# Attention and a soft mixture of experts on one core: longer q and k loads, transposes on quarters, one-bank tail tiles, zero products on TensorE

## The chip, the cores and the metric

The kernel runs on one core of a Trainium2 chip. The metric is the device time of one execution in microseconds. Times are medians of several executions; "span" is the part of an execution that the profile covers, about 1.8 us shorter than its time. All ratios are the mean time of one kernel's fast runs over the mean of the other's fast runs in the same rounds, so they are not quite the ratio of the medians quoted beside them.

Terms: TensorE makes the matrix products and writes them to tiles in PSUM, a memory of eight banks here; VectorE and ScalarE copy them out, which is called eviction. A load "lands" when its last bytes have arrived. A packet is one piece of a transfer, as the page counts them. The transfers are spread over 16 DMA engines; "DMA share" is their mean busy share, and "clock" the part of its full clock that TensorE was granted (PEclk in the strips, in tenths).

## The reference

```python
# attention: q, k, v are (4, 8, 768, 64); heads 0, 2, 6 see all earlier keys,
# the others the first 4 keys and the last 64
scores = scale * np.matmul(q, k.transpose(0, 1, 3, 2))
scores = np.where(mask, scores, -1e9)
a = softmax(scores)
x = np.matmul(a, v)                      # -> (3072 tokens, 512)
# soft mixture of experts, 8 experts with 4 slots each
logits = x @ phi                         # (3072, 32)
slot_input = softmax_over_tokens(logits).T @ x
for e in range(8):                       # w1[e]: 512 x 1024, w2[e]: 1024 x 512
    slot_out[e] = np.maximum(slot_input[e] @ w1[e], 0.0) @ w2[e]
return softmax_over_slots(logits) @ slot_out        # (3072, 512), f32
```

Nothing of the output can be written before the softmax over all tokens is done and all eight second-layer weights have been used. The inputs are 52.5 MB of f32, cast to bf16 on the way in (26.25 MB); the output is 6.29 MB.

## The kernel before

The parts that the change and the argument touch, with cuts marked `# ...`. `NP` is 16 pairs of heads; `trp`, `pvp` and `scp` are PSUM pools of two tiles each (one bank, one bank, two banks, eight banks in all).

```python
    def load_qk(n, which):
        # ...
        t = raw.tile([P, 2, 384], BF16, tag="r" + which, name="r" + which)
        nc.gpsimd.dma_start(t, src[b, h:h + 2].rearrange("h (p s) d -> p h (s d)", s=6))

    def transposes(n, which):
        # ...
        for s in range(6):
            for hh in range(2):
                nc.tensor.transpose(tp[64 * hh:64 * hh + 64, s, :], src[:, hh, 64 * s:64 * s + 64], ident)
    # ...
    for h in range(H):      # far masks, before the first exponential
        nc.scalar.copy(fmask[:, h], r1[:, h:h + 1]...to_broadcast([P, 4, 66]))
        nc.scalar.copy(fmask[:, h, 0], r0[:, h:h + 1].to_broadcast([P, 66]))
    # ... sixteen pairs of attention, with weights loaded between q, k and v; then the experts' tail ...
    sp = pvp.tile([P, DM], F32, tag="pv", name="sp")
    for e4, gs in ((0, (0, 1, 2, 3)), (1, (0, 1)), (1, (2,)), (1, (3,))):
        second(e4, gs)                              # the last group waits for the last weights
    V.tensor_copy(slot_out[:, :256], sp[:, :256])
    nc.scalar.copy(slot_out[:, 256:], sp[:, 256:])

    for t, rows in enumerate((1, 1, 2, 4, 4, 4, 4, 4)):
        ot = single([P, rows, DM], F32, f"ot{t}", tag=f"w1_{t}")
        for y in range(0, rows, 2):
            op = scp.tile([P, 2, DM], F32, tag="sc", name="op")
            for x in range(min(2, rows)):
                nc.tensor.matmul(op[:, x], er[r], slot_out, start=True, stop=True)
                if r % 2:
                    nc.scalar.activation(ot[:, y + x], op[:, x], ACT.Copy, scale=rrow[:, r:r + 1])
                else:
                    V.tensor_scalar(ot[:, y + x], op[:, x], rrow[:, r:r + 1], None, op0=ALU.mult)
                r += 1
        nc.sync.dma_start(ov[:, r - rows:r, :], ot)
```

The softmax here doesn't subtract the row's maximum and nothing guards it: scores larger than these inputs give would overflow.

## Time and profile before

| | before |
|---|---|
| time, median (lowest to highest) | 169.53 us (168.79 to 169.67, 3 runs) |
| span of the profiled run | 168.9 us (an execution of 170.73 us) |
| attention's last exponential and products end | about 117 us |
| last weights land | 139.1 us |
| slot_out ready | 141.05 us |
| output written, end | 168.9 us |

Read it as two stages that cannot overlap: loads until the last weights have landed, and the output after slot_out. Attention lies inside the first. What each stage costs is set by what ends last in it, not by the busiest engine: the page's first part (below: engine, busy us, share of the span, instructions) has no engine above 72%.

```profile
PE 121.2 (72%) x1751; PEld 72.0 (43%) x1752; DVE 102.0 (60%) x226; ACT 113.7 (67%) x162; POOL 58.6 (35%) x89
```

The wait of the output queue's own engine (SPq; line 523 is where the program ends) for its last transfer is short, 3.4 us: it is handed its last rows late.

```profile
SPq L523 <- DMA out_dram<-ot: 3.4, 1, 3.4
```

### The profile page before, as it was taken

The page shows a single profiled execution, that of the slowest core. Times are in us where ns is not written, and L with a number is a line of the kernel's source. Part 1 is how long each engine was busy: PE and PEld are TensorE (multiplying, and loading weights), DVE is VectorE, ACT ScalarE, POOL GpSimd, SP SyncE. Part 2 cuts the span into 40 slices and gives each one's busy share as a digit, 9 for nine tenths or more (in the row PEclk, how much of TensorE's full clock was granted, in tenths as well). Part 3 has the DMA queues.
Part 4 walks back from the last instruction along what each step waited for, and adds up shares of the span by engine and source line. Part 5 has one row for each costly group of instructions (what it writes and reads, how often), then busy time and mean ns, then how long its engine had stood idle before and what let it go on. Part 6 is the DMA issues. An engine that isn't in the chain of part 4 may idle for free.

```text
span 168.9 us, 4098 instructions
## 1 busy us (share of the span) xinstructions
PE 121.2 (72%) x1751; PEld 72.0 (43%) x1752; DVE 102.0 (60%) x226; ACT 113.7 (67%) x162; POOL 58.6 (35%) x89
## 2 busy tenths in 40 slices
PE   0445988987769989869989887988587964565430
PEld 0332555654436556546565545556233721111100
DVE  2846579999657889755898765887224104434410
ACT  3599899999778999978999979792303202334330
POOL 7974475463644445544453615006100000000000
PEclk9999999999999999995999997899858997555555
DMA  3999999999999999999999999999999920556665
GB/s 46 150 175 187 200 194 197 190 215 189 202 196 196 209 196 192 201 201 200 201 196 192 211 191 212 213 215 216 210 213 217 205 50 28 220 237 260 248 278 219
DMA packets 39985, 32.80 MB, mean 194 GB/s; under 512 B 26656, under 2 KB 34848, under 8 KB 39328
## 3 DMA queue, kind: packets, MB, share of 16 engines
q0 software_dynamic: 38672, 26.25, 104.4%
q1 hardware_dynamic: 1296, 6.30, 9.2%
q8 instruction: 13, 0.21, 0.5%
q14 instruction: 4, 0.03, 0.0%
HBM read 52.50 MB, written 6.29 MB: 348 GB/s over the span
## 4 chain that ended last, share of the span: by engine, by line
DMA 36%; PE 8%; DVE 8%; issue 3%; POOL 1%; ACT 1%; POOLq 0%
DMA w<-in_moe_w_dram 29%; DMA rk<-in_k_dram 7%; PE op L486 7%; DVE ot L490 5%; DVE pT L183 1%; PE sp L470 1%; DVE Tq L147 1%; POOL vb L114 0%; ACT ot L488 0%; DVE xb L201 0%; POOL w L127 0%; POOL w L391 0%; PE pv L192 0%; DVE xT L210 0%; DVE slot_out L476 0%
## 5 line engine op out<-in xcount | busy, mean ns | idle before, releaser
L171 ACT ACTIVATE pT<-sc 128x1024 bf16<-128x1024 f32 (+1 forms) x96 | 83.6, 928 | 9.3 <-PE sc L166 8.6
L166 PE MATMUL sc<-Tq,Tk 64*128 64x256 bf16 (+3 forms) x320 | 37.4, 300 | 16.6 <-ACT Tk L150 8.9
L192 PEld LDWEIGHTS <-pT 128*128 128x128 bf16 x672 | 25.1, 100 | 11.2 <-issue 7.9
L183 DVE TENSOR_TENSOR pT<-pT,msk 128x1024 bf16<-128x1024 bf16 (+1 forms) x48 | 29.3, 639 | 0.2 <-ACT pT L171 0.2
L192 PE MATMUL pv<-vb,pT 128*128 128x65 bf16 x352 | 27.7, 198 | 0.0
L192 PE MATMUL pv<-vf,pT 128*128 128x65 bf16 x320 | 25.3, 197 | 0.0
L114 POOL DMA_DIRECT2D vb<-in_v_dram x16 | 16.5, 1034 | 22.8 <-PE sc L166 7.7
L166 PEld LDWEIGHTS <-Tk 64*128 64x128 bf16 x320 | 12.1, 96 | 27.4 <-ACT Tk L150 11.6
L486 PE MATMUL op<-slot_out,expT 128*128 128x512 bf16 x23 | 11.7, 599 | 11.0 <-DVE ot L490 10.1
L147 DVE COPY Tq<-tpq 128x768 bf16<-128x768 bf16 x16 | 15.3, 957 | 5.5 <-PE tpq L140 5.5
L201 DVE TENSOR_TENSOR xb<-pv,rs 128x384 bf16<-128x384 f32 x32 | 17.8, 558 | 1.1
L488 ACT ACTIVATE ot<-op,rrow 128x512 f32<-128x512 f32 x12 | 8.3, 688 | 14.4 <-PE op L486 14.4
L200 DVE RECIPROCAL rs<-pv 128x6 f32<-128x6 f32 x32 | 6.2, 194 | 18.9 <-PE pv L192 18.7
L490 DVE TENSOR_SCALAR ot<-op,rrow 128x512 f32<-128x512 f32 x12 | 9.0, 751 | 12.7 <-PE op L486 12.7
L150 ACT COPY Tk<-tpk 128x768 bf16<-128x768 bf16 x16 | 13.0, 814 | 3.8 <-PE tpk L140 3.8
L108 POOL DMA_DIRECT2D rk<-in_k_dram x16 | 11.5, 719 | 7.4 <-PE sc L166 3.2
L140 PE MATMUL tpk<-ident,rk 128*64 128x128 bf16 x192 | 9.4, 240 | 5.5 <-DMA rk<-in_k_dram 4.9
L108 POOL DMA_DIRECT2D rq<-in_q_dram x16 | 11.5, 717 | 2.1 <-DMA vb<-in_v_dram 1.9
L140 PE MATMUL tpq<-ident,rq 128*64 128x128 bf16 x192 | 10.0, 251 | 3.0 <-DMA rq<-in_q_dram 3.0
L127 POOL DMA_DIRECT2D w<-in_moe_w_dram x16 | 9.0, 561 | 8.1 <-DMA w<-in_moe_w_dram 7.2
L486 PEld LDWEIGHTS <-expT 128*128 128x128 bf16 x24 | 3.8, 157 | 17.6 <-issue 17.5
L140 PEld LDWEIGHTS <-rk 128*64 128x64 bf16 x192 | 6.7, 120 | 9.5 <-DMA rk<-in_k_dram 4.9
(70 smaller groups left out, 118.1 us busy)
## 6 DMA issues: line engine op xcount, KB each, us to landing
w<-in_moe_w_dram POOLq DMA_DIRECT2D x32, 512.0 KB, 12.5
out_dram<-ot SPq DMA_DIRECT2D x5, 1024.0 KB, 3.9
rk<-in_k_dram POOLq DMA_DIRECT2D x16, 192.0 KB, 11.5
rq<-in_q_dram POOLq DMA_DIRECT2D x16, 192.0 KB, 11.5
vb<-in_v_dram POOLq DMA_DIRECT2D x16, 192.0 KB, 10.8
out_dram<-ot SPq DMA_DIRECT2D x2, 256.0 KB, 2.2
out_dram<-ot SPq DMA_DIRECT2D x1, 512.0 KB, 2.6
phi<-in_moe_phi_dram POOLq DMA_DIRECT2D x1, 32.0 KB, 10.4
```

What stands on the lines that cost most here:

```text
L108: nc.gpsimd.dma_start(t, src[b, h:h + 2].rearrange("h (p s) d -> p h (s d)", s=6))
L114: nc.gpsimd.dma_start(vbs[n % 5].rearrange("p h j d -> p (h j) d")[:, :, :D], a.rearrange("h (j p) d -> p (h j) d", p=P))
L140: nc.tensor.transpose(tp[64 * hh:64 * hh + 64, s, :], src[:, hh, 64 * s:64 * s + 64], ident)
L147: nc.vector.tensor_copy(o, i)
L150: nc.scalar.copy(o, i)
L166: nc.tensor.matmul(sc[:, hh, at:at + 128 * cnt], kT[n][po:po + 64, j * 128:(j + 1) * 128], qT[n][po:po + 64, i0 * 128:(i0 + cnt) * 128], s ...
L171: nc.scalar.activation(pT[n][:, :, o:o + ln], sc[:, :, :ln], ACT.Exp, scale=scale)
L183: nc.vector.tensor_mul(x, x, m)
L192: nc.tensor.matmul(pv[n][:, i % 3, hh, :], pT[n][:, hh, o:o + 128], vv[:, hh, j, :D + 1], start=(j == 0), stop=(j == i))
L201: nc.vector.tensor_mul(xb[b][:, 3 * half:3 * half + 3, h * D:(h + 2) * D].rearrange("p i (h d) -> p i h d", h=2), pv[n][:, :, :, :64], rs. ...
L486: nc.tensor.matmul(op[:, x], er[r], slot_out, start=True, stop=True)
L490: V.tensor_scalar(ot[:, y + x], op[:, x], rrow[:, r:r + 1], None, op0=ALU.mult)
```

## The change

Its intent: fewer and longer DMA runs for q and k (128 rows of 3 KB, two heads on two halves of the partitions, so that each head's transposes use a diagonal quarter of the array); loads issued in the order of need; the far masks taken off ScalarE, which had to finish them before its first exponential; in the tail one-bank tiles, so that two engines and two neighbours in time don't share a tile; and products with zeros where TensorE would wait, to hold its clock.

```diff
-        t = raw.tile([P, 2, 384], BF16, tag="r" + which, name="r" + which)
-        nc.gpsimd.dma_start(t, src[b, h:h + 2].rearrange("h (p s) d -> p h (s d)", s=6))
+        t = raw.tile([P, S], BF16, tag="r" + which, name="r" + which)
+        nc.gpsimd.dma_start(t, src[b, h:h + 2].rearrange("h (p s) d -> (h p) (s d)", s=12))
 ...
-        for s in range(6):
+        for s in range(12):
             for hh in range(2):
-                nc.tensor.transpose(tp[64 * hh:64 * hh + 64, s, :], src[:, hh, 64 * s:64 * s + 64], ident)
+                po = slice(64 * hh, 64 * hh + 64)
+                nc.tensor.transpose(tp[po, s, :], src[po, 64 * s:64 * s + 64], ident[po, po])
 ... (order of loads: q before k, v and weights after them)
+    def keep_busy(t, count):
+        for _ in range(count):
+            nc.tensor.matmul(t, zero[:, :P], zero, start=True, stop=True)
 ... (31 such products: 9 + 10 around the start, 12 in the tail)
-        nc.scalar.copy(fmask[:, h], r1[:, h:h + 1]...)          # all 8 heads at the start
+        V.tensor_copy(fmask[:, h:h + 2, 1:], r1[:, h:h + 2]...)  # 2 heads, as needed
 ... (slot sums in three bf16 tiles; hp, transposes of h and sp in one-bank tiles;
      the second layer in two halves of 256 columns; row sums rp after second(1, (0, 1)))
-    V.tensor_copy(slot_out[:, :256], sp[:, :256])
-    nc.scalar.copy(slot_out[:, 256:], sp[:, 256:])
+    V.tensor_copy(slot_out[:, :256], sp[0])
+    nc.scalar.copy(slot_out[:, 256:], sp[1])
 ...
-        for y in range(0, rows, 2):
-            op = scp.tile([P, 2, DM], F32, tag="sc", name="op")
-            for x in range(min(2, rows)):
-                nc.tensor.matmul(op[:, x], er[r], slot_out, start=True, stop=True)
+        for y in range(rows):
+            op = bank((1, 2, 0)[r % 3])        # one bank, six tiles in rotation
+            nc.tensor.matmul(op, er[r], slot_out, start=True, stop=True)
```

More of the change, by code (lines that the diff above doesn't have):

```diff
@@ L87 @@
     slot_acc = single([P, DM], F32, "slot_acc")
-    slot_bf = single([P, 2, DM], BF16, "slot_bf")
+    slot_bf = [single([P, DM], BF16, f"slot_bf{x}") for x in range(3)]
     xT = single([P, 4, S], BF16, "xT")
@@ L112, in load_v @@
         b, h = n // 4, 2 * (n % 4)
-        a = v[b, h:h + 2]
         nc.gpsimd.dma_start(vbs[n % 5].rearrange("p h j d -> p (h j) d")[:, :, :D],
-                            a.rearrange("h (j p) d -> p (h j) d", p=P))
+                            v[b, h:h + 2].rearrange("h (j p) d -> p (h j) d", p=P))
     wi = [0]
@@ L136, in transposes @@
         src = (qraw if which == "q" else kraw)[n]
-        tp = trp.tile([P, 6, P], BF16, tag="tr", name="tp" + which)
-        for s in range(6):
+        tp = trp.tile([P, 12, 64], BF16, tag="tr", name="tp" + which)
+        for s in range(12):
             for hh in range(2):
-                nc.tensor.transpose(tp[64 * hh:64 * hh + 64, s, :], src[:, hh, 64 * s:64 * s + 64], ident)
+                po = slice(64 * hh, 64 * hh + 64)
+                nc.tensor.transpose(tp[po, s, :], src[po, 64 * s:64 * s + 64], ident[po, po])
         return tp
@@ L144, in evac @@
         dst = qkT.tile([P, S], BF16, tag="T" + which, name="T" + which)
-        o, i = dst.rearrange("c (p s) -> c p s", s=6), tp.rearrange("c s p -> c p s")
+        o, i = dst.rearrange("c (p s) -> c p s", s=12), tp.rearrange("c s p -> c p s")
         if which == "q":
@@ L237, in dispatch_mm @@
     def dispatch_mm(b, i0=0, i1=6):
-        if i0 == 0:
-            sps[b] = pvp.tile([P, DM], F32, tag="pv", name="slp")
+        sp = sps[b, i0] = pvp.tile([P, DM], F32, tag="pv", name="slp")
         for i in range(i0, i1):
-            g = i % 4
-            nc.tensor.matmul(sps[b][32 * g:32 * g + 32, :], elgs[b][:, i, :], xb[b][:, i, :],
-                             start=(i < 4), stop=(i + 4 >= 6))
+            g = (i - i0) % 4
+            nc.tensor.matmul(sp[32 * g:32 * g + 32, :], elgs[b][:, i, :], xb[b][:, i, :],
+                             start=(i - i0 < 4), stop=(i + 4 >= i1))
     def slot_sum(b):
-        sp = sps[b]
+        sp = sps[b, 0]
         if b == 0:
@@ L249, in slot_sum @@
         elif b == B - 2:
-            nc.vector.tensor_add(slot_bf[:, 0], slot_acc, sp)
-        elif b < B - 1:
+            nc.vector.tensor_add(slot_bf[0], slot_acc, sp)
+        else:
             nc.vector.tensor_add(slot_acc, slot_acc, sp)
-        else:
-            nc.scalar.copy(slot_bf[:, 1, :256], sp[:, :256])
-            nc.vector.tensor_copy(slot_bf[:, 1, 256:], sp[:, 256:])
     load_qk(0, "k")
@@ L264 @@
                    allow_small_or_imprecise_dtypes=True)
+    load_qk(1, "q")
+    load_qk(1, "k")
     load_v(0)
-    load_qk(1, "k")
-    load_qk(1, "q")
+    w_load(1)
+    load_qk(2, "q")
+    load_qk(2, "k")
     load_v(1)
     w_load(1)
-    load_qk(2, "k")
-    load_qk(2, "q")
     load_v(2)
-    w_load(1)
     V = nc.vector
+    zero = single([P, 512], BF16, "zero")
+    V.memset(zero, 0.0)
+    def keep_busy(t, count):
+        for _ in range(count):
+            nc.tensor.matmul(t, zero[:, :P], zero, start=True, stop=True)
+    idle = pvp.tile([P, 512], F32, tag="pv", name="idle")
+    keep_busy(idle, 9)
     V.tensor_single_scalar(ident, diff[:, :P], 0.0, op=ALU.is_equal)
@@ L297, with far_mask @@
         evac(0, which, transposes(0, which))
+        keep_busy(idle, 2)
     for h in range(2):
         head_mask(h)
-    V.memset(vbs[0][:, :, :, D:], 1.0)
-    for h in range(H):
-        nc.scalar.copy(fmask[:, h], r1[:, h:h + 1].rearrange("p (o d) -> p o d", o=1).to_broadcast([P, 4, 66]))
-        nc.scalar.copy(fmask[:, h, 0], r0[:, h:h + 1].to_broadcast([P, 66]))
-    for t in vbs[1:]:
+    def far_mask(n):
+        h = 2 * n
+        V.tensor_copy(fmask[:, h:h + 2, 1:], r1[:, h:h + 2].rearrange("p (h a d) -> p h a d", a=1, d=1).to_broadcast([P, 2, 3, 66]))
+        V.tensor_copy(fmask[:, h:h + 2, 0], r0[:, h:h + 2].rearrange("p (h d) -> p h d", d=1).to_broadcast([P, 2, 66]))
+    for t in vbs:
         V.memset(t[:, :, :, D:], 1.0)
+    far_mask(0)
     def setup_late():
@@ L319 @@
         if n + 3 < NP:
+            load_qk(n + 3, "q")
             load_qk(n + 3, "k")
-            load_qk(n + 3, "q")
             load_v(n + 3)
@@ L332 @@
         scores(n, 0)
+        if n == 0:
+            keep_busy(idle, 2)
         if n >= 1:
@@ L347 @@
         scores(n, 2)
+        if n == 0:
+            keep_busy(idle, 2)
         if n >= 1:
@@ L361 @@
         scores(n, 4)
+        if n == 0:
+            keep_busy(idle, 2)
         if n + 1 < NP:
@@ L378 @@
         if n < 3:
+            far_mask(n + 1)
             for h in (2 * n + 2, 2 * n + 3):
@@ L387 @@
     w2s[5] = single([P, 8, DM], BF16, "w2_5", tag="msk")
-    def w2_late(e):
-        for half in range(2):
-            nc.gpsimd.dma_start(w2s[e][:, 4 * half:4 * half + 4], w2v[e][:, 4 * half:4 * half + 4])
-    w2_late(5)
+    nc.gpsimd.dma_start(w2s[5], w2v[5])
     w2s[6] = ptp.tile([P, 8, DM], BF16, tag="pT", name="w2_6")
-    w2_late(6)
+    nc.gpsimd.dma_start(w2s[6], w2v[6])
     last, bl = NP - 1, B - 1
@@ L407 @@
     w2s[7] = ptp.tile([P, 8, DM], BF16, tag="pT", name="w2_7")
-    w2_late(7)
+    for half in range(2):
+        nc.gpsimd.dma_start(w2s[7][:, 4 * half:4 * half + 4], w2v[7][:, 4 * half:4 * half + 4])
+    idle = scp.tile([P, 512], F32, tag="sc", name="idle")
     x_transpose(last, 0, 3)
+    keep_busy(idle, 2)
     logits_mm(bl, (3,), (0,))
@@ L412 @@
     x_transpose(last, 3, 6)
+    keep_busy(idle, 1)
     logits_mm(bl, (3,), (1,))
     logits_exp(bl, 1)
+    keep_busy(idle, 1)
     exp_tokens(bl, 0, 3)
+    keep_busy(idle, 1)
     dispatch_mm(bl, 0, 3)
+    keep_busy(idle, 1)
     exp_tokens(bl, 3, 6)
+    keep_busy(idle, 1)
     dispatch_mm(bl, 3, 6)
-    slot_sum(bl)
+    keep_busy(idle, 3)
+    V.tensor_copy(slot_bf[1][:96], sps[bl, 0][:96])
+    V.tensor_copy(slot_bf[2][:96], sps[bl, 3][:96])
     csum = small.tile([P, 1], F32, tag="cs", name="csum")
@@ L424, with bank @@
     V.tensor_scalar(emask, emask, rcol, None, op0=ALU.mult)
-    sip = trp.tile([P, 4, ES], F32, tag="tr", name="sip")
-    sv = [slot_bf[:, x].rearrange("p (di do) -> p do di", do=4) for x in range(2)]
+    def bank(t, shape=(P, 512), dt=F32):
+        pool, tag = ((scp, "sc"), (trp, "tr"), (pvp, "pv"))[t]
+        return pool.tile(list(shape), dt, tag=tag, name="bank")
+    sip = bank(1, (P, 4, ES))
+    sv = [t.rearrange("p (di do) -> p do di", do=4) for t in slot_bf]
     for do in range(4):
-        for x in range(2):
-            nc.tensor.matmul(sip[:, do], sv[x][:, do], sum4, start=(x == 0), stop=(x == 1))
+        for x in range(3):
+            np_ = 96 if x else P
+            nc.tensor.matmul(sip[:, do], sv[x][:np_, do], sum4[:np_], start=(x == 0), stop=(x == 2))
@@ L432 @@
     V.tensor_copy(siT, sip)
+    keep_busy(idle, 2)
     hs = []
     for e4 in range(2):
-        hp = scp.tile([P, 2, 512], F32, tag="sc", name="hp")
+        t = xp.tile([P, 2, 512], BF16, tag="xb", name="hs")
         for c in range(2):
+            hp = bank(0 if e4 == 0 else 2)
             for do in range(4):
                 for g in range(4):
-                    nc.tensor.matmul(hp[32 * g:32 * g + 32, c], siT[:, do],
+                    nc.tensor.matmul(hp[32 * g:32 * g + 32], siT[:, do],
@@ L440 @@
                                      w1s[4 * e4 + g][:, do, c * 512:(c + 1) * 512],
                                      start=(do == 0), stop=(do == 3))
-        t = xp.tile([P, 2, 512], BF16, tag="xb", name="hs")
-        nc.scalar.activation(t[:, 0], hp[:, 0], ACT.Relu, scale=emask[:, e4:e4 + 1])
-        V.tensor_scalar(t[:, 1], hp[:, 1], emask[:, e4:e4 + 1], 0.0, op0=ALU.mult, op1=ALU.max)
+            if c == 0:
+                nc.scalar.activation(t[:, 0], hp, ACT.Relu, scale=emask[:, e4:e4 + 1])
+            else:
+                V.tensor_scalar(t[:, 1], hp, emask[:, e4:e4 + 1], 0.0, op0=ALU.mult, op1=ALU.max)
@@ L445 @@
         hs.append(t.rearrange("p c f -> p (c f)").rearrange("p (fi fo) -> p fo fi", fo=8))
-    hT = []
-    for e4 in range(2):
-        tp = trp.tile([P, 8, P], BF16, tag="tr", name="tph")
-        for fo in range(8):
-            nc.tensor.transpose(tp[:, fo, :], hs[e4][:, fo, :], ident)
-        t = qkT.tile([P, 8, P], BF16, tag="hT", name="hT")
-        if e4 == 0:
-            V.tensor_copy(t, tp)
-        else:
-            nc.scalar.copy(t, tp)
-        hT.append(t)
-    rp = trp.tile([P, 24], F32, tag="tr", name="rp")
+    hT = {}
@@ new lines, in turn, with second @@
+    def turn(e4):
+        t = qkT.tile([P, 8, P], BF16, tag="T" + "qk"[e4], name="hT")
+        for x in range(2):
+            tp = bank(1, (P, 4, P), BF16)
+            for fo in range(4):
+                nc.tensor.transpose(tp[:, fo, :], hs[e4][:, 4 * x + fo, :], ident)
+            if x:
+                nc.scalar.copy(t[:, 4:], tp)
+            else:
+                V.tensor_copy(t[:, :4], tp)
+        hT[e4] = t
+    sp = [bank(0, (P, 256)) for x in range(2)]
+    def second(e4, gs):
+        for fo in range(8):
+            for x in range(2):
+                for g in gs:
+                    nc.tensor.matmul(sp[x][32 * g:32 * g + 32, :], hT[e4][:, fo, 32 * g:32 * g + 32],
+                                     w2s[4 * e4 + g][:, fo, 256 * x:256 * x + 256],
+                                     start=(e4 == 0 and fo == 0), stop=(e4 == 1 and fo == 7))
@@ L458 @@
+    turn(0)
+    second(0, (0, 1, 2, 3))
+    turn(1)
+    second(1, (0, 1))
+    rp = bank(1, (P, 24))
     er = []
@@ L463 @@
     V.reciprocal(rrow, rp)
-    sp = pvp.tile([P, DM], F32, tag="pv", name="sp")
-    def second(e4, gs):
-        for fo in range(8):
-            for g in gs:
-                nc.tensor.matmul(sp[32 * g:32 * g + 32, :], hT[e4][:, fo, 32 * g:32 * g + 32],
-                                 w2s[4 * e4 + g][:, fo, :],
-                                 start=(e4 == 0 and fo == 0), stop=(e4 == 1 and fo == 7))
-    for e4, gs in ((0, (0, 1, 2, 3)), (1, (0, 1)), (1, (2,)), (1, (3,))):
-        second(e4, gs)
-    V.tensor_copy(slot_out[:, :256], sp[:, :256])
-    nc.scalar.copy(slot_out[:, 256:], sp[:, 256:])
+    second(1, (2,))
+    second(1, (3,))
+    V.tensor_copy(slot_out[:, :256], sp[0])
+    nc.scalar.copy(slot_out[:, 256:], sp[1])
     ov = out.rearrange("(p r) d -> p r d", r=24)
@@ L482 @@
         ot = single([P, rows, DM], F32, f"ot{t}", tag=f"w1_{t}")
-        for y in range(0, rows, 2):
-            op = scp.tile([P, 2, DM], F32, tag="sc", name="op")
-            for x in range(min(2, rows)):
-                nc.tensor.matmul(op[:, x], er[r], slot_out, start=True, stop=True)
-                if r % 2:
-                    nc.scalar.activation(ot[:, y + x], op[:, x], ACT.Copy, scale=rrow[:, r:r + 1])
-                else:
-                    V.tensor_scalar(ot[:, y + x], op[:, x], rrow[:, r:r + 1], None, op0=ALU.mult)
-                r += 1
+        for y in range(rows):
+            op = bank((1, 2, 0)[r % 3])
+            nc.tensor.matmul(op, er[r], slot_out, start=True, stop=True)
+            if r % 2:
+                nc.scalar.activation(ot[:, y], op, ACT.Copy, scale=rrow[:, r:r + 1])
+            else:
+                V.tensor_scalar(ot[:, y], op, rrow[:, r:r + 1], None, op0=ALU.mult)
+            r += 1
         nc.sync.dma_start(ov[:, r - rows:r, :], ot)
```

## The prediction

> **What bounds the kernel now.** I read the page first: its strip of 40 slices (each 4.2 us) and the shares of the chain of work that ended last.
>
> ```profile
> PEclk9999999999999999995999997899858997555555
> DMA  3999999999999999999999999999999920556665
> GB/s 46 150 175 187 200 194 197 190 215 189 202 196 196 209 196 192 201 201 200 201 196 192 211 191 212 213 215 216 210 213 217 205 50 28 220 237 260 248 278 219
> ...
> DMA 36%; PE 8%; DVE 8%; issue 3%; POOL 1%; ACT 1%; POOLq 0%
> ```
>
> The DMA engines are full from slice 2 to slice 32, then almost empty for two slices, then 50 to 60% busy to the end. So there are two stages: loading (to about 139 us), limited by transfers, and writing out (141 us on), limited by something else. The chain in order of time names the links:
>
> ```profile
> 87.81 13.67 DMA w<-in_moe_w_dram
> ...
> 101.77 15.23 DMA w<-in_moe_w_dram
> ...
> 119.73 19.38 DMA w<-in_moe_w_dram
> ...
> 139.15 1.04 PE sp L470 x4
> ...
> 140.21 0.43 DVE slot_out L476
> ...
> 140.67 0.38 ACT slot_out L477
> ...
> 160.50 1.03 PE op L486 x2
> ...
> 161.55 0.76 DVE ot L490
> ...
> 162.97 0.69 ACT ot L488
> ```
>
> From 75 us on it is load after load; the last expert weights land at 139.1 us, four matmuls follow, and then two matmuls alternate with one eviction until 163.7 us. The waits say why:
>
> ```profile
> PE op L486 <- DVE ot L490: 10.1, 12, 0.8
> ...
> ACT slot_out L477 <- DVE slot_out L476: 8.2, 1, 8.2
> ```
>
> Before each pair of output rows TensorE waits 0.8 us for the eviction of an earlier pair, because a pair shares one two-bank tile. ScalarE likewise starts its half of slot_out only after VectorE's half. Busy time by windows (columns: stretch, length, PE, PEld, DVE, ACT, POOL, PE clock, DMA share, GB/s) gives the transfer rates:
>
> ```profile
> 80.00:90.00 10.00, 8.86 (x166) 5.57 (x163) 8.61 (x20) 9.54 (x13) 4.80 (x8) 1.00 1.48 197
> ...
> 112.00:114.00 2.00, 1.63 (x26) 0.97 (x22) 1.66 (x5) 2.00 (x4) 0.00 (x0) 1.00 1.05 211
> ```
>
> ```profile
> 152.00:153.00 1.00, 0.24 (x1) 0.00 (x0) 0.72 (x1) 0.54 (x1) 0.00 (x0) 0.50 0.09 33
> ...
> 165.00:166.00 1.00, 0.00 (x0) 0.00 (x0) 0.00 (x0) 0.00 (x0) 0.00 (x0) 0.50 0.95 393
> 166.00:167.00 1.00, 0.00 (x0) 0.00 (x0) 0.00 (x0) 0.00 (x0) 0.00 (x0) 0.50 0.96 393
> ```
>
> Loads count bytes as written (bf16; twice as many are read). With q, k and v in the mix they run at 197 GB/s, with weights alone at 211 to 217. Output writes reach 393 to 460 GB/s when rows are ready, and pause when they are not. ScalarE is at 95% in the attention stage, but attention ends near 118 us and the weights land 21 us later: its pace is beside the path.
>
> **What the Trainium skill says.** "DMA: Bandwidth & Descriptors", section "Why small descriptors are slow (HBM only)": a packet pays a fixed overhead of about 3 cycles beside one per 32 bytes. The trace agrees in direction (197 against 211 to 217). "PSUM — Partial Sum Buffer", section on bank collisions: two engines must not be on one bank and quadrant at once; the wait of slot_out's two halves, which share a bank, is what that looks like. "TensorE: Matmul & The Clock Gate", Part 1: the array falls to half clock after an idle window of about 3.4 us; the strip shows 5 from 141 us on, and the windows 0.50 from 122 to 126 us. "TensorEngine Tiling (Array Packing)", Key Properties: different tiles load weights and multiply in parallel; no run of before shows this for 64 by 64 quarters.
>
> **Loads as longer rows.** q and k go from 256 runs per tile of 1.5 KB read and 0.75 KB written to 128 of twice that: 32 tiles x 128 = 4096 packets fewer, 256 per DMA engine. v keeps its 24,576 packets of 128 bytes, the larger part. The cost of a packet, estimated: an attention iteration lasts about 6.4 us, so it moves 6.4 x 197 = 1.26 MB, which at 213 would take 5.92 us. The missing 0.48 us falls on the 2048 q, k and v packets of a pair, 128 per engine: 3.75 ns each. 256 x 3.75 = **1.0 us** saved in total. The skill's 3 cycles agree, as an estimate: 3 of 51 cycles before, 3 of 99 after, so 3% of the 29 us that 12.6 MB of q and k reads take at 428 GB/s, 0.9 us. The order of the loads doesn't change their sum, and the queue is full in either order. So the last weights land near 138.1 us.
>
> **ScalarE's masks.** Sixteen casts (8 x 0.407 + 8 x 0.246 = 5.2 us) hold the first exponential until 11.25 us, although its scores were there by about 9. Moved to VectorE, in four parts, they let attention start about 2 us earlier. That is beside the path: it turns into idle time before the last weights.
>
> **Transposes on quarters.** Twelve of 128 rows become 24 of 64 by 64. In the iteration from 83.4 us twelve took 0.46 us, 38 ns each. If the small ones also need 38 ns, an iteration gains 2 x 0.46 = 0.9 us of TensorE, against 0.84 us in which TensorE sat idle there for ScalarE. If two quarters run side by side, nothing. At worst some 0.1 to 0.4 us an iteration, 2 to 6 us by the end of attention, of which the earlier start gives back 2.
>
> **Zero products and one-bank tiles before the end.** At 123.4 us 64 matmuls of the first expert layer took 5.7 us, mostly at half clock; at full clock I take 74 ns each (20 took 1.48 us after 127.6), 4.7 us or less. Evictions by bank let the transposes start after the first half. I estimate 3 to 4 us off this stage, minus 0.5 us for the third slot_bf copy. Before, TensorE was done at 137.7 us with all that it had weights for, 1.4 us ahead of the landing. Now it should be about as far ahead or further, so again the **landing decides: 0 us**. In splitting the second layer into halves of 256 columns the number of matmuls doubles, but the columns don't.
>
> **slot_out in two banks.** The 0.38 us of ScalarE falls beside VectorE's 0.43 us: **0.4 us** saved with the gap between them.
>
> **Output rows in six one-bank tiles.** Now 27.85 us pass from slot_out (141.05) to the end (168.9). With six tiles in rotation matmuls follow each other at 0.43 us (half clock), 24 in 10.3 us; VectorE needs 12 x 0.75 = 9.0, ScalarE 12 x 0.69 = 8.3. A row of 256 KB needs 0.65 us of DMA at 400 GB/s. So the **transfer is the new bound**: 6.29 MB / 400 = 15.7 us. Before it: 0.04 + 0.45 + 0.75 + 0.9 (issue to first bytes, 142.4 to 143.2 us in the old trace) = 2.15 us; one gap of 0.4 us before the first 1 MB; after the last bytes 1.9 us, as now (167.0 to 168.9). Sum 20.15 us, **7.7 us** saved.
>
> **Sum:** 1.0 + 0 + 0.4 + 7.7 = 9.1 us. 169.5 - 9.1 = **160.4 us**.
>
> **Rivals.** (1) Transposes or extra zero products slow TensorE, so that compute and not the last weights ends the loading stage. For it: ScalarE and TensorE are both nearly full in attention, and TensorE's margin at the landing is only 1.4 us. Against: the faster tail and the earlier start give 5 us of room. It would make 162 to 164 us. (2) The output stays short of rows, or one core's writes sustain less than 400 GB/s when continuous: at 350 they take 18 us, total 162.7. For it: the clock is still half there. Against: 0.43 us a row is well below 0.65, and windows of 2 us at 393 and more exist. (3) The loads gain more: from 134.5 to 139.1 us the rate falls from 205 to 8 GB/s, so some DMA engines end 3 us after the mean. If fewer packets shrink that tail, 157 to 158 us. If the loads gain nothing, 161.4.
>
> **Range and chances.** The output stage alone brings 4 to 5%, and its mechanism is a repeated wait of 0.8 us in plain view; both bad rivals together leave about 165. Range 157 to 164; faster by over 2%: 0.95, within 2%: 0.04, slower: 0.01.
>
> **What would show it.** Right: q0 has some 4,100 packets fewer; the last weight lands 0.5 to 2 us before 139.1; TensorE is idle just before it; the wait of op for ot is gone or harmless; DMA share near 1 through the output; slot_out to end about 20 us. Wrong: a chain through PE or ACT, not DMA, at 130 us (rival 1); DMA share well under 0.9 with rows waiting, or 350 GB/s at full share (rival 2); a landing before 136 us (rival 3). A load stage that gets longer, by transfers held back for buffers, would break the prediction.

## The result, and the profile after

The changed kernel took 159.95 us (median of 4 runs, 159.22 to 160.22) against 169.6 us in the same rounds; ratio 0.9424, 95% interval 0.9367 to 0.9481. Run again later in six runs it took 160.06 us, ratio 0.9453 (0.9406 to 0.9501).

The page's strip and the queue's packets after (the strip's slices are 3.9 us now):

```profile
PEclk9999579999997899999689999999999999999755
DMA  3999999999999999999999999999999999339995
GB/s 39 165 170 192 189 197 189 205 198 208 196 195 204 200 207 200 191 205 201 206 200 193 203 202 204 200 214 214 214 215 220 224 204 203 63 119 416 427 419 212
...
q0 software_dynamic: 34288, 26.25, 108.2%
```

The loading stage looks as before, a little shorter. The two thin slices between the stages remain. Then the output stage is three slices at 416 to 427 GB/s and parts of two others, where it was six of 219 to 278. The queue had 38,672 packets before: 4096 fewer from q and k, 288 fewer from two weight loads that are no longer split.

The chain in order of time (start, length, what):

```profile
116.38 20.92 DMA w<-in_moe_w_dram
...
137.34 1.05 PE bank L495 x8
...
138.41 0.38 ACT slot_out L513
...
138.84 0.40 PE bank L521
...
139.27 5.45 DVE ot L525 x9
```

Set this beside the chain of before: the last weights land at 137.30 in place of 139.11 us; the two halves of slot_out now end together, 1.49 us after the landing and not 1.94; and the evictions follow each other without a matmul between them, because the next row is already in another bank.

The waits (engine and line, for whom, total us, times, longest):

```profile
PE bank L495 <- DMA w<-in_moe_w_dram: 0.8, 1, 0.8
```

```profile
SPq L558 <- DMA out_dram<-ot: 8.9, 1, 8.9
```

TensorE still waits for the last weights, but only 0.8 us, where it had waited 1.4. And the output queue, which had its last rows late, now has issued everything by 147.65 us and waits 8.9 us for its last transfer: the output is bound by its transfers. Busy time by windows, two from its start and one from its end, shows the same:

```profile
141.00:142.00 1.00, 0.91 (x4) 0.39 (x3) 1.00 (x3) 1.00 (x3) 0.00 (x0) 1.00 1.02 381
142.00:143.00 1.00, 0.89 (x4) 0.52 (x4) 1.00 (x2) 1.00 (x3) 0.00 (x0) 1.00 1.05 414
...
155.00:156.00 1.00, 0.00 (x0) 0.00 (x0) 0.00 (x0) 0.00 (x0) 0.00 (x0) 0.50 0.94 393
```

DMA share is close to 1 (0.94 to 1.15 in windows of 1 us) from the first bytes (140.9 us) to the last (156.0): 6.29 MB in 15.1 us, 417 GB/s. The PE clock (the third figure from the right) is full where I had expected half.

| | before | after | difference |
|---|---|---|---|
| last weights land | 139.11 | 137.30 | -1.8 |
| landing to slot_out ready | 1.94 | 1.49 | -0.45 |
| slot_out ready to end | 27.85 | 19.1 | -8.75 |
| span | 168.9 | 157.9 | -11.0 |

The two profiles differ by 11.0 us but the timed runs by 9.4 to 9.7. The profiled execution of before took 170.7 us, one of its slower ones. So single profiles can't size a term of 1 us; the runs below show how far a landing moves.

### The profile page after: what moved, and what is told of

It reads as the page before. It is cut to its first block, busy times and chain, and to the rows that moved or that the text cites. A ratio compares the mean times of both kernels' runs of the same rounds, so it can differ in the third digit from the quotient of the medians.

```text
span 157.9 us, 5077 instructions
## 1 busy us (share of the span) xinstructions
PE 124.7 (79%) x2235; PEld 79.4 (50%) x2235; DVE 104.4 (66%) x237; ACT 108.3 (69%) x146; POOL 51.8 (33%) x87
## 3 DMA queue, kind: packets, MB, share of 16 engines
HBM read 52.50 MB, written 6.29 MB: 372 GB/s over the span
## 5 line engine op out<-in xcount | busy, mean ns | idle before, releaser
L166 PEld LDWEIGHTS <-Tk 64*128 64x128 bf16 x320 | 11.4, 95 | 23.8 <-ACT Tk L150 9.9
L147 DVE COPY Tq<-tpq 128x768 bf16<-128x768 bf16 x16 | 15.3, 956 | 3.8 <-PE tpq L140 3.4
L108 POOL DMA_DIRECT2D rk<-in_k_dram x16 | 8.7, 541 | 11.8 <-DMA vb<-in_v_dram 2.8
L277 PE MATMUL idle<-zero 128*128 128x512 bf16 x31 | 10.9, 452 | 1.2 <-DVE zero L273 1.2
L140 PEld LDWEIGHTS <-rk 64*64 64x64 bf16 x384 | 7.9, 112 | 6.4 <-issue 5.7
L140 PE MATMUL tpk<-ident,rk 64*64 64x64 bf16 x384 | 9.4, 197 | 1.9 <-DVE Tq L147 1.9
L108 POOL DMA_DIRECT2D rq<-in_q_dram x16 | 8.6, 540 | 6.6 <-PE sc L166 4.8
L140 PE MATMUL tpq<-ident,rq 64*64 64x64 bf16 x384 | 9.9, 203 | 1.1 <-DMA rq<-in_q_dram 1.1
L140 PEld LDWEIGHTS <-rq 64*64 64x64 bf16 x384 | 8.1, 117 | 5.1 <-issue 2.7
L210 DVE COPY xT<-tpx 128x768 bf16<-128x768 bf16 (+1 forms) x17 | 9.0, 529 | 1.6 <-PE tpx L209 1.6
L209 PE MATMUL tpx<-ident,xb 128*128 128x128 bf16 x96 | 8.9, 230 | 0.5 <-DVE xb L201 0.3
```

What stands on the lines that cost most here:

```text
L140: nc.tensor.transpose(tp[po, s, :], src[po, 64 * s:64 * s + 64], ident[po, po])
L147: nc.vector.tensor_copy(o, i)
L166: nc.tensor.matmul(sc[:, hh, at:at + 128 * cnt], kT[n][po:po + 64, j * 128:(j + 1) * 128], qT[n][po:po + 64, i0 * 128:(i0 + cnt) * 128], s ...
L210: nc.vector.tensor_copy(xT[:, hp, i0 * 128:i1 * 128], tp[:, i0 * 128:i1 * 128])
L277: nc.tensor.matmul(t, zero[:, :P], zero, start=True, stop=True)
```

## The experiments

Theory 1 (the prediction's): the load stage ends with the landing of the last weights, the output stage had been paced by evictions of row pairs and is now paced by transfers; fewer packets bring 1 us, output rows 7.7, the rest nothing. Rivals: compute, not the landing, ends the load stage, so that the masks, the zero products and the tail's tiles carry the gain; or the full clock in the output carries it.

**Output rows alone.**

```diff
 # before.py
-        for y in range(0, rows, 2):
-            op = scp.tile([P, 2, DM], F32, tag="sc", name="op")
+        for y in range(rows):
+            pool, tag = ((trp, "tr"), (pvp, "pv"), (scp, "sc"))[r % 3]
+            op = pool.tile([P, DM], F32, tag=tag, name="op")
```

> The kernel before with one part of the change alone: each output row has a one-bank tile of its own, in rotation over the six tiles of three pools; slot_out, loads and zero products as before. My theory (the output stage was paced by evictions in pairs and becomes a transfer of 6.29 MB at about 400 GB/s): slot_out to the end takes 20 us in place of 27.9, the time falls by 7.5 to 8.7 us, at half PE clock still. Rival (the half clock or the rows' supply still limits the writes, and the zero products that kept the clock full are what helped): DMA share well below 0.9 in the output, gain of 4 us or less.

Measured: 161.65 us against 169.59, ratio 0.9507 (0.9445 to 0.9568): 8.4 us. From slot_out (140.69) to the end (160.3) it took 19.6 us, with DMA share near 1 from 143 us on. The clock was half up to the window of 144 to 145 us, and the stage was only 0.5 us longer than in the changed kernel. Two windows of this run:

```profile
143.00:144.00 1.00, 1.00 (x4) 0.34 (x2) 0.83 (x2) 0.84 (x2) 0.00 (x0) 0.50 1.00 371
144.00:145.00 1.00, 1.00 (x4) 0.49 (x3) 0.90 (x2) 0.83 (x2) 0.00 (x0) 0.64 1.05 418
```

So the rotation of one-bank tiles alone is nearly all of the gain, and the clock is not its cause. The run changes two things at once, one row for a tile and six tiles in place of two; how the gain divides between them no run shows.

**q and k rows alone.** The first two parts of the diff above, put into the kernel before.

> The kernel before with q and k as 128 rows of 3 KB and the 24 transposes on diagonal quarters, nothing else. My theory (4096 packets fewer, 3.75 ns each per engine): the last weights land about 1.0 us before 139.1 and the time falls by about 1 us. Rival A (fewer packets also shrink the spread between DMA engines at the end of the loads): 1.8 to 3 us. Rival B (smaller transposes cost TensorE more than they save, 24 at 38 ns, 0.9 us an iteration): attention ends later than 118 us, by up to 6 us, with no gain in time.

Measured: 167.94 us, ratio 0.9882 (0.9827 to 0.9936): 2.0 us, 1.1 to 2.9. The last weights landed at 137.4 us. More than the 1.0 of theory 1, with 1.0 just outside the interval; rival A is favoured. Rival B is out: attention's last product started at 117.0 us, against 116.6 in the profile of before. TensorE's order of time shows why. First the kernel before, then the changed kernel, each with the transposes of one q tile and the scores that follow (start, length, line, operation, count):

```profile
84.48 0.53 PE L140 MATMUL tpq<-ident,rq 128*64 128x128 bf16 x12
84.94 0.34 PE L166 MATMUL sc<-Tq,Tk 64*128 64x256 bf16 x4
```

```profile
83.78 0.56 PE L140 MATMUL tpq<-ident,rq 64*64 64x64 bf16 x24
...
84.28 0.34 PE L166 MATMUL sc<-Tq,Tk 64*128 64x256 bf16 x4
```

From the first transpose to the first score it took 0.46 us before and 0.50 after: 24 small ones cost 21 ns each, a little over half of the old 38. So they cost TensorE next to nothing. Why each is so short is not shown: the two quarters may run side by side, but a small transpose also has 64 columns to pass in place of 128 (the last shapes in the two lines), which could explain it without that.

**Everything but the output rows.**

```diff
 # after.py
-        for y in range(rows):
-            op = bank((1, 2, 0)[r % 3])
+        for y in range(0, rows, 2):
+            op = scp.tile([P, 2, DM], F32, tag="sc", name="op")
```

> The changed kernel with its output rows in pairs on two-bank tiles as before, everything else as changed. My theory: nearly all of the gain goes, slot_out to the end takes 26 to 28 us again, less than before only by what the full PE clock gives (0.2 us a matmul, 24 matmuls, at most half of it in the chain), time 165.5 to 168. Rival (the full clock alone would have helped the old pairs): 162 to 164.

Measured: 168.76 us (one of the four runs slow), ratio of the fast runs 0.9917 (0.9814 to 1.0019): against 0.9424, 8.4 us of the gain are gone. slot_out to the end took 27.1 us again, although the clock was full until 143 us. In this profile TensorE was last in the load stage: the loads' last bytes came at 136.7 us and slot_out at 139.2. That was the first sign that theory 1's "the landing decides" holds by a small margin only.

**No zero products.**

```diff
     def keep_busy(t, count):
-        for _ in range(count):
-            nc.tensor.matmul(t, zero[:, :P], zero, start=True, stop=True)
+        return
```

> The changed kernel without any of the zero products (33 matmuls of 512 columns fewer), everything else as changed. My theory (the landing of the last weights decides the load stage, and transfers the output): no change beyond 0.5 us, though the PE clock falls to one half around 120 to 128 us and in the output. Rival (the tail's compute has so little room, some 0.5 us before the landing in the changed kernel, that a half clock makes it the last): 1 to 4 us slower.

(It is 31 products, not 33.) Measured: 160.12 us (159.59 to 161.71), ratio 0.9438 (0.9366 to 0.9509): no difference from the changed kernel that the runs can show. But the mechanism of the rival is there. Windows of the changed kernel, then of this one:

```profile
123.00:125.00 2.00, 2.00 (x44) 0.96 (x36) 0.75 (x1) 0.69 (x1) 0.00 (x0) 1.00 1.04 217
```

```profile
123.00:125.00 2.00, 1.62 (x26) 0.71 (x27) 0.53 (x3) 0.00 (x0) 0.00 (x0) 0.50 1.00 209
```

Without the zeros the first expert layer runs at half clock: its 64 matmuls take 5.78 us, not 3.64. In the profiled execution, at 161.7 us the slowest of the four, compute was last, with slot_out at 140.8 us; the three others took 159.6 to 160.4. The output stage took 19.1 us here too.

**q and k as before in the changed kernel.** The load and the transposes of the kernel before, in the changed kernel.

> The changed kernel with q and k as before (256 runs of 1.5 KB, 12 transposes of 128 rows), everything else as changed. Theory A (the loads end the stage, and 4096 packets cost 1 to 2 us): last weights land near 138.5 to 139, time 161 to 162, 1 to 2 us above the changed kernel. Theory B (by now compute ends the stage about as often as the landing, as the run without zero products showed): less than 1 us above it, or none, because the shorter transposes give TensorE back what the loads lose.

Measured: 160.97 us (six runs, 159.75 to 161.82), ratio 0.9481 (0.9428 to 0.9534). Against 0.9424 and 0.9453 for the changed kernel that is 0.5 to 1 us, and the intervals overlap. The landing was at 139.3 us in the profile. Theory B fits better, but the run doesn't decide by itself.

The landings of all profiles together do more. I take two figures from windows of 0.1 us: the end of the last one with any load bytes, and a mean end, 130.5 us plus the time that the bytes after it would need at 213 GB/s.

| q and k | profiles | last bytes (range) | mean end (range) |
|---|---|---|---|
| 256 runs of 1.5 KB | 3 | 138.2 us (137.3 to 138.7) | 135.94 us (135.91 to 135.97) |
| 128 rows of 3 KB | 8 | 136.9 us (136.1 to 138.1) | 134.96 us (134.62 to 135.31) |

The mean end moves by 0.98 us, which is the 1.0 us worked out from 3.75 ns a packet. The last bytes move by 1.3 us, but that figure scatters by 2 us between executions, since it belongs to the slowest of 16 engines (the DMA share in the last microsecond of the loads was 0.04 before, less than one engine in 16).

**v in long rows too.** This takes the loads off the path.

```diff
-        nc.gpsimd.dma_start(vbs[n % 5].rearrange("p h j d -> p (h j) d")[:, :, :D],
-                            v[b, h:h + 2].rearrange("h (j p) d -> p (h j) d", p=P))
+        vlong[n] = raw5.tile([P, S], BF16, tag="rv", name="rv")
+        nc.gpsimd.dma_start(vlong[n], v[b, h:h + 2].rearrange("h (p s) d -> (h p) (s d)", s=12))
 ... (the near blocks read one tile of ones, the far product reads vlong)
```

> Wrong results on purpose: the changed kernel with v loaded as 128 rows of 3 KB into tiles that are read only by the far product; the near blocks read ones. It has 22,500 packets fewer (1408 per engine) for the same bytes. At my estimate of 3.75 ns a packet the last weights land 5.3 us earlier, near 132. Theory A (the landing alone decides): the time falls by about 5 us to 155. Theory B (compute is right behind the landing): the landing moves by 4 to 6 us but the time falls by 1.5 us at most, and the chain runs through TensorE.

Measured: 158.8 us (158.32 to 159.87), ratio 0.9368 (0.9313 to 0.9423), results wrong as intended. The loads' mean end fell to 130.6 us, 4.4 us earlier: 3.1 ns for each of 1408 packets per engine. The last bytes came by 131.75 us. Yet the time fell by only about 1.2 us (1.0 and 1.4 by the ratios 0.9424 and 0.9453 of the changed kernel, whose intervals overlap with this one). Its chain, then its windows:

```profile
132.50 1.76 PE bank L510 x24
...
134.25 3.19 PE bank L497 x32
...
137.47 0.38 ACT slot_out L515
```

```profile
132.00:133.00 1.00, 1.00 (x18) 0.78 (x13) 0.00 (x0) 0.00 (x0) 0.00 (x0) 1.00 0.00 0
...
136.00:137.00 1.00, 1.00 (x13) 0.89 (x10) 0.00 (x0) 0.00 (x0) 0.00 (x0) 1.00 0.00 0
```

From 132 us the DMA engines are empty and TensorE is busy until slot_out: row sums, then the second layer's last products. Theory B is shown: compute stands about 1 us behind the landing (slot_out at 137.85 us, against 138.8 in the changed kernel), and theory 1's picture of ample idle time ahead of it is gone.

**The far masks on ScalarE as before.**

```diff
-    far_mask(0)
+    for h in range(H):
+        nc.scalar.copy(fmask[:, h], r1[:, h:h + 1]...)
+        nc.scalar.copy(fmask[:, h, 0], r0[:, h:h + 1]...)
```

> The changed kernel with the far masks cast by ScalarE at the start as before (16 casts, 5.2 us), everything else as changed. Prediction's theory (beside the path): no change beyond 0.5 us. Theory B (compute is co-critical): attention starts about 2 us later (first exponential near 10.5 in place of 8.1), and of that 0.8 us lie in the wait for the weights, so 1 to 1.5 us slower, near 161.

Measured: 160.03 us (five runs, 159.5 to 161.56), ratio 0.9418 (0.9359 to 0.9477): no change. Attention's last product started at 115.7 us, in the changed kernel's two profiles at 115.1 and 116.5.

**The loads in the old order.** v before the next pair's k and q at the start, k before q in the loop.

> The changed kernel with the loads issued in the old order (v before the next pair's k and q at the start, k before q), everything else as changed. My prediction's theory (the sum of the loads is the same, the start is beside the path): no change beyond 0.5 us, though attention starts its second pair 1 to 2 us later. Rival (that start is on the compute chain, which is last in some executions): up to 1 us slower.

Measured: 159.88 us, ratio 0.9421 (0.9372 to 0.947): no change. So three parts of the change, taken out one at a time (the zero products, the masks and the order), bring nothing that can be measured here.

**The experts' tail as before.** The lines from the first expert layer to slot_out are those of the kernel before (two-bank and whole-bank tiles, second layer 512 columns wide).

> The changed kernel with the part from the first expert layer to slot_out as before (two-bank and whole-bank tiles, second layer 512 columns wide, slot_out from one bank in turn), everything else as changed, zero products and output rows included. Prediction's theory: only slot_out's 0.4 us is lost. Theory B: compute reaches the last weights 1 to 2 us later, which is more than the 0.8 us of room, so 1 to 2.5 us slower in all.

Measured: 161.14 us, ratio 0.9494 (0.944 to 0.9548), about 0.7 to 1.2 us above the changed kernel, with intervals that just overlap. TensorE waited 2.2 us for the last weights, so its work before them was not longer; what was longer came after: from the landing (137.45) to slot_out (139.56) 2.1 us in place of 1.5. That is 0.6 us, slot_out's halves in turn and the last products. The output took 19.5 us in place of 19.1, at half clock until 145 us. The rest is within the scatter. Theory B's mechanism is not what this run shows; on the contrary, the old tail brought TensorE to the last weights earlier. The second layer's products here (start, length, line, operation, count), then the first two of their three groups in the run with long v loads, which has the new tail and waits for no loads (the third, 134.25 us, is in its chain above):

```profile
130.41 4.87 PE L496 MATMUL sp<-w,hT 128*32 128x512 bf16 x60
137.49 1.20 PE L496 MATMUL sp<-w,hT 128*32 128x512 bf16 x4 [2.20 <-DMA w<-in_moe_w_dram]
```

```profile
127.73 1.93 PE bank L497 x64
...
130.58 1.92 PE bank L497 x32
```

Old tail 4.87 + 1.20 = 6.07 us, new tail 1.93 + 1.92 + 3.19 = 7.04 us, both at full clock. So the halves of 256 columns, with the row sums between them, cost about 1 us more for the same columns.

**Row sums in place of zeros, a candidate for something better.** If compute stands close behind, 1.8 us of it (the 24 row-sum products of one column each, placed before the last weights) could be moved to the gaps that the zero products fill.

```diff
-    keep_busy(idle, 1)      # after exp_tokens(bl, 3, 6)
+    row_sums(0, 6)
     dispatch_mm(bl, 3, 6)
-    keep_busy(idle, 3)
+    row_sums(6, 18)
 ... (after the slot inputs: row_sums(18, 24) in place of keep_busy(idle, 2))
```

> A candidate for something better: the changed kernel with the 24 row-sum matmuls (1.8 us of TensorE just before the last weights) moved to where TensorE waits for other engines after the last exponentials, in place of three groups of zero products. Theory (landing and compute end within a microsecond or two of each other, whichever is later counts): compute reaches the last weights 1.5 us sooner, which helps only in executions where compute was last, so 0 to 0.8 us faster than the changed kernel. Rival (the landing alone decides): no change. Rival (one-column products don't hold the clock): half clock near 122 us and 1 us slower.

Measured: 160.58 us, ratio of the fast runs 0.9453 (0.9405 to 0.9501), exactly that of the changed kernel in the same rounds. One of its six executions took 505 us, with TensorE's products several times as long throughout; it counts as slow, and nothing is concluded from it. (The profile of this version is of that execution, so its stages can't be read.)

> Wrong results on purpose: the long v loads and the early row sums together. With the loads out of the way the chain is TensorE's, so the moved 1.8 us should now count: 1.2 to 1.8 us faster than the run with long v loads alone (158.8), about 157.2. If it stays at 158.8, something other than TensorE's work in the tail sets the end there.

Measured with the long v loads (wrong): 157.63 us (157.38 to 159.44), ratio 0.9316 (0.9261 to 0.937), 0.9 us below the long v loads alone, with intervals that overlap. In the profiles this comes from attention, whose last product started 1.6 us earlier (114.2 against 115.8); from there to slot_out it took 22.6 us, not 22.0. The reason is in its window:

```profile
123.00:125.00 2.00, 2.00 (x24) 0.76 (x20) 0.00 (x0) 0.69 (x1) 0.00 (x0) 0.50 1.01 209
```

Half clock: the first expert layer took 6.32 us in place of 3.64, although TensorE had hardly stood still before it. In the run with long v loads alone, with its zero products in place, the same window shows 1.00. So here the one-column products didn't hold the clock as the 512-column products with zeros had done. What the move saved it lost again. This also shows that the zero products do what they are for; in the changed kernel it rarely reaches the end.

**The changed kernel again.**

> The changed kernel as it is, on the same chip and in the same rounds as the others, to compare with directly and to see how far its last landing and its attention's end move between executions: 159.5 to 160.3, landing between 136 and 138.5, attention's last matmul between 115 and 117.

Measured: 160.06 us (159.57 to 161.62); landing at 137.3 us in its profile too. No version beat the changed kernel with right results.

## Why the prediction was right

- **Output rows: 7.7 us predicted, 8.4 us alone (8.75 in the profiles).** The mechanism, evictions that hold up TensorE because two rows share a tile, was right and confirmed both ways, by putting the new rows in alone and by taking them out alone. But the wait was misread: it doesn't stand before each pair, for an earlier one. Odd rows are ScalarE's in the code, and in the old profile VectorE evicts row 22 from 161.55 to 162.31 us, TensorE starts row 23 of the same pair at 162.35, and ScalarE evicts that from 162.97. So the second row of a pair waited for the eviction of the first, though it goes to the tile's other bank; this accounts for eleven of the twelve waits. The term was mis-sized by two of its parts: the transfer went at 417 GB/s, not 400 (15.1 us, not 15.7), and the gap of 0.4 us before the first large transfer didn't come. Rows came at eviction pace, as the clock was full where I had put half.
- **Loads: 1.0 us predicted.** The mean end of the loads moved by 0.98 us over eleven profiles, and 1408 packets fewer per engine moved it 4.4 us, 3.1 ns each, against my 3.75. What I had not put into the sum but among the rivals is the spread between engines; with it the last bytes moved 1.3 us, and the part alone was worth 2.0 us (1.1 to 2.9).
- **slot_out: 0.4 us predicted, 0.45 in the profiles.** The run with the old tail lost 0.6 us after the landing.
- **Masks, order, transposes: 0 predicted, 0 measured.** For the transposes the estimate of 0 to 0.46 us a tile was 0.04; that two quarters run side by side, the reason given for 0, is not shown.
- **"The landing decides: 0 us".** The sum came out, but the step failed as a picture, so its 0 is partly luck. I expected TensorE at least 1.4 us ahead of the landing, with the faster tail and the earlier start as room. It was 0.8 and 0.2 us ahead in the changed kernel's two profiles, behind in those of two variants (pairs back, no zero products), and with the loads 4.4 us shorter only about 1.2 us were gained. Both sources of room had been overrated.
  - The tail: 3 to 4 us were to come off. From the start of the first layer to the end of the second layer's products TensorE needed 15.3 us before (without its wait for weights) and 14.5 with the new tail (the run with long v loads), 0.8 us less. The first layer took 3.64 us and not 5.70, but the second took 7.04 and not 5.76: that splitting it leaves the number of columns as it was didn't keep it from costing more. Its halves and the row sums now between them came together; no run separates them fully, though with the sums moved away its last 64 products took 4.58 us in place of 1.92 + 3.19.
  - The start: the first exponential came at 8.12 us in place of 11.25, but at the ninth pair 0.8 us of the lead was left (its k is evicted from 60.94 us, before from 61.72). Attention's last product starts anywhere from 114.2 to 117.1 us in these profiles, with or without the masks. Why it moves so is open; the profiles show stretches of half clock at different places, which fits, but no run isolated it.
- **The clock in the output: wrong.** It was full from slot_out to 148 us. It didn't matter, since transfers bound that stage.

By parts: rows 8.4 us, q and k 2.0, sum 10.4, against 9.3 to 9.8 for the whole by the ratios; the tail's 0.7 to 1.2 and the rest are within the intervals. The excess is within them too. It would fit that shorter loads soon meet compute (q and k brought 2.0 us in the old kernel, 0.5 to 1 in the new one), but that isn't shown.

## What to carry to other kernels

Look for engines that take turns on one PSUM tile at the end of a kernel: a wait of 0.8 us repeated twelve times was worth more than everything else here, and six one-bank tiles turned an eviction pace into a transfer pace. Follow each wait to the row that it waits for: here two rows in different banks of one tile held each other up. Work out what the next bound is, and take the landing of the last load out once in an experiment, results wrong or not: it shows how much compute stands behind it before effort goes into loads. And compare several profiles before sizing a term of 1 us.

## What the Trainium skill lacked or had wrong

- "TensorE: Matmul & The Clock Gate", Part 1, gives an idle window of about 3.4 us as what lets the clock fall, and reports that frequent short idles can do it too. Here it fell without such a window: in the kernel before at about 121 us, after gaps of at most 0.5 us in the 4 us before, and with one-column products in place of zero products at about 120 us (0.50 from 121 to 125 us), after one gap of 0.3 us. How full the array must be kept, the page doesn't say, and these runs don't measure it.
- "DMA: Bandwidth & Descriptors", "Why small descriptors are slow (HBM only)": its 3 cycles a packet agree roughly with the runs (3.1 ns a packet measured with the long v loads; as an estimate, 3 times 32 bytes at 428 GB/s, twice the 214 GB/s written, over 16 engines take 3.6 ns). It does not give the spread: the last engine's bytes came 1.2 to 2.8 us after the mean end of a load stage of 132 us.
- The same page's "Measured" table has loads only. Here stores in 8 KB runs, by one core alone, went at 417 GB/s over 15.1 us; the page has a figure above its ~358 GB/s limit only for loads by one core.
- "TensorEngine Tiling (Array Packing)", Key Properties, says that tiles run in parallel, and that a change of the tiling mode drains the array. For transposes on two diagonal 64 by 64 quarters the runs add a number: 24 in 0.50 us, against 12 of 128 rows in 0.46. They don't tell whether the quarters ran in parallel, nor what a drain at the change of mode cost.
